# Earlier w_out conversions, and block 0's routing spread over eight ticks of block 1's layer

## Chip, cores and metric

The kernel runs on one core of a Trainium2 chip. The metric is the device time of one execution in microseconds (us), the median over the runs.

## What is computed

Three stages follow one another. Windowed attention (4 batches, 8 heads, 576 positions, head size 64) gives x with 2304 rows of 512. A gated layer with 1536 hidden units follows, and a soft mixture of 8 experts with 4 slots each.

```python
scores = np.where(masks, scale * q @ k.T, -1e9)
x = softmax(scores) @ v                                   # 2304 x 512
x = (1/(1+np.exp(-(x @ w_gate))) * (x @ w_val)) @ w_out   # 1536 hidden
logits = x @ phi                                          # 32 slots
slot_input = softmax(logits, axis=0).T @ x
slot_out = relu(slot_input @ w1[e]) @ w2[e]               # per expert e
out = softmax(logits, axis=1) @ slot_out
```

## The kernel before

The 2304 rows of x are cut into blocks 0 to 3 of 512 rows and block 4 of 256. The product with w_out is never made for x: w_out times phi is made once (`slot_weights`, into `wp`), the logits come from the hidden units g and `wp`, and g itself is gathered into the slots.

Of the gated layer a block has 12 steps f, each of 128 hidden units and two halves (`l1`: gate, then value, 12 matmuls each). Weights are split in two parts (`whl`: high and low, `split_w`, lines 492 and 493: ScalarE casts, GpSimd or VectorE subtracts). The raw weights must first be converted (`convert`, lines 438 to 441: ScalarE, VectorE twice, and an add on GpSimd, for each of two halves). Twelve conversions are for w_gate and w_val and are done along block 0's layer; six, number 12 to 17 of the order `turn`, are for w_out. The steps after which these six stand are in `WO_AT`, where 12 is the first step of block 1. Each calls `slot_weights`, whose four parts (two turns, `wt_ps`; a product, `pt_ps`; a sum, `wp_ps`) come 3 to 6 ticks later. A tick (`on_tick`) is one half of a step.

After each half `between` is called. `sab` there adds the attention of blocks 1 to 4, in 8 pairs of units: scores (`s_ps`), softmax (VectorE, ScalarE and, line 387, a scale on GpSimd), transposes (`tr`, line 187), weighted sums (`xp`, line 207). The last pair's keys are loaded into a buffer that the transposes of the pair before free.

`Post(n)` is the routing of block n, in 18 steps: logits (`lt_ps`), 12 turns of g (`tp`, line 816, four transposes each, copied into `gt` by VectorE or ScalarE in turn), weights (`dt_ps`), 3 gathers (`sp`, line 847), and the shares of the second softmax (`c_ps`, lines 873 to 890). `Spread(steps, marks)` gives out steps call by call.

Blocks 2 and 3 are done together (`pair_l1`) with sums and differences of their halves. What they need is made between block 1's layer and the pair: splits of x (`b_hi`, `b_lo`, `b`), eight sums on GpSimd (`tsum`, line 576), splits of these (`t_hl`, lines 552 and 553), and weights with their sums (`w_`, `s`, lines 612 to 640). This list, `prep`, is mixed with what is left of block 0's routing and with block 1's, so that the list ends 3 steps before the routing does. The cast at line 640 makes the high part of the second weights of the pair's first step. This stretch is called the passage below.

The order on each engine is set by a scheduler that goes by the order of the code and by when it believes an instruction's operands to be ready. The score, turn and sum matmuls of the pairs, the early loads and the prepared lists are kept in the order of the code. On each engine the instructions then run in the order given.

Of the kernel before, what the change touches and what calls it, by code (L numbers as in the profile page):

```python
# [22 lines left out]
NF = 12  # L23
HIP = 200
LA = 2
WO_AT = (12, 13, 14, 15, 16, 17)
WARM = 8
SMALL = 70
GA = 1
# [25 lines left out]
def pb_tokens(n):  # L55
    return 512 if n < 4 else 256
# [3 lines left out]
def tile_kernel(  # L60
# [25 lines left out]
    def b8(tag, shape, dt, name):  # L86
        return big.tile(shape, dt, tag=tag, name=name, bufs=BUFS[tag])
# [146 lines left out]
    def ld(ins):  # L234
        return tc.keep_in_program_order(ins) if early[0] else ins
# [172 lines left out]

    wo_at = {z: i for i, z in enumerate(WO_AT)}
    turn = [0, 1]  # L410
# [5 lines left out]
    def stage(z):  # L416
        if z in staged:
            return
        staged[z] = b8("l2", [P, 1024, 2], U32, "st")
        ld(nc.sync.dma_start(staged[z].rearrange("p a b -> p (a b)"), wd[z].bitcast(U32)))  # L420

    def store():
        while stores:
            ld(nc.sync.dma_start(*stores.pop(0)))

    def convert(z):
        i = n_conv[0]
        n_conv[0] += 1
        stage(z)
        if i + 1 < len(turn):  # L430
            stage(turn[i + 1])
        st = staged[z]
        store()
        fw = b8(("ws", "ws", "gb", "xt")[i % 4] if i < NF else ("gb", "xt")[i % 2], [P, 2, 1024], F32, "fw")
        for h in range(2):
            c = slice(512 * h, 512 * h + 512)
            top, low = fw[:, 0, c], fw[:, 1, c]
            nc.scalar.activation(top, st[:, c, 1].bitcast(F32), AF.Prelu, scale=2.0**-112, alpha=2.0**32)  # L438
            nc.vector.tensor_scalar(top.bitcast(U32), top.bitcast(U32), 3, None, ALU.logical_shift_left)
            nc.vector.tensor_scalar(low.bitcast(I32), st[:, c, 0], 2.0**-29, None, ALU.mult)  # L440
            nc.gpsimd.tensor_tensor(low.bitcast(I32), top.bitcast(I32), low.bitcast(I32), ALU.add)  # L441
        if z < NF:
            stores.append((wg32[z // 2][:, z % 2], fw[:, 1]))
        else:
            y = z - NF
            stores.append((wo32[y // 2][:, 2 * (y % 2) : 2 * (y % 2) + 2].rearrange("p a c -> p (a c)"), fw[:, 1]))
            slot_weights(2 * y, fw[:, 1].rearrange("p (c x) -> p c x", c=2), 3)
        return fw[:, 1]
# [4 lines left out]
    def on_tick():  # L453
        ticks[0] += 1
        for x in [x for x in later if x[0] <= ticks[0]]:
            later.remove(x)
            x[1](*x[2])

    def slot_weights(f, wo_f, lag):

        wt = pm.rearrange("p a b -> p (a b)").rearrange("p (k c x) -> p k c x", k=ND, c=2)
        at_ = {}

        def turned(c):
            wt_ps = ps_a.tile([P, ND, P], F32, tag="a", name="wt_ps")
            for kc in range(ND):
                nc.tensor.transpose(wt_ps[:, kc], wo_f[:, c, P * kc : P * kc + P], ident)  # L467
            nc.scalar.copy(wt[:, :, c], wt_ps)

        def product():  # L470
            pt_ps = ps_m.tile([P, 2, P], F32, tag="m", name="pt_ps")
            for kc in range(ND):
                nc.tensor.matmul(
                    pt_ps[32 * kc : 32 * kc + 32], lhsT=phi[:, kc, :], rhs=wt[:, kc], start=True, stop=True
                )
            at_["pt"] = cpool.tile([P, 2, P], F32, tag="pt", name="pt")
            nc.vector.tensor_copy(at_["pt"], pt_ps)

        def summed():
            wp_ps = ps_m.tile([P, 2, 32], F32, tag="m", name="wp_ps")  # L480
            for c in range(2):
                nc.tensor.matmul(wp_ps[:, c], lhsT=at_["pt"][:, c], rhs=i4, start=True, stop=True)
            nc.vector.tensor_copy(wp[:, f : f + 2], wp_ps)

        for n, (step, *args) in enumerate(((turned, 0), (turned, 1), (product,), (summed,))):
            later.append((ticks[0] + lag + n, step, args))

    def split_w(src, pool=(True, False)):
        whl = b8("w", [P, 2, 2, ND, P], F32R, "whl")
        src = src.rearrange("p (a k c) -> p a k c", a=2, k=ND)  # L490
        for h in range(2):
            nc.scalar.copy(whl[:, 0, h], src[:, h])  # L492
            (nc.gpsimd if pool[h] else nc.vector).tensor_tensor(  # L493
                whl[:, 1, h], src[:, h], whl[:, 0, h].bitcast(F32), ALU.subtract
            )
        return whl
# [17 lines left out]
    def l1(n, f, whl, between):  # L514
        nt = pb_tokens(n)
        per = 2048 // nt
        tag = {0: "ga", 1: "gb", 4: "xt" if f < per else "xb"}[n]
        if (n, f // per) not in g_cur:
            g_cur[n, f // per] = b8(tag, [P, per, nt], F32, "g")
        g = g_cur[n, f // per][:, f % per]  # L520
        for a in range(2):
            pt = ps_l1.tile([P, 512], F32, tag="l1", name="l1ps")
            first = True
            for dc in HP_ORDER:
                for w_, x_ in ((0, x_hi), (0, x_lo), (1, x_hi)):
                    nc.tensor.matmul(  # L526
                        pt[:, 0:nt],
                        lhsT=whl[:, w_, a, dc, :],
                        rhs=x_[n][:, dc, :],
                        start=first,  # L530
                        stop=(dc == HP_ORDER[-1] and w_ == 1),
                    )
                    first = False
            with tc.high_priority(offset=HIP):
                if a == 0:
                    nc.scalar.activation(g, pt[:, 0:nt], AF.Sigmoid)  # L536
                else:
                    nc.vector.tensor_tensor(g, pt[:, 0:nt], g, ALU.mult)  # L538
            between()
        g_sb[n, f] = g  # L540
# [401 lines left out]
    def ahead(z):  # L942
        if z < NF:
            conv[z] = convert(z)

    for z, (fn, *args) in enumerate(first_attn(lambda: stage(0))):
        fn(*args)
        if z == C0:
            sab = Pairs()
# [5 lines left out]
    def load_w(z):  # L955
        if z < NF // 2:
            wst[z] = b8("ws", [P, 2, 1024], F32, "wst")
            ld(nc.sync.dma_start(wst[z], wg32[z]))

    for f in range(NF):  # L960
        whl = split_w(conv.pop(f), SPL)
        ahead(f + LA)
        if f >= 10:
            store()
            load_w(f - 10)
        l1(0, f, whl, sab)
    after = Post(0).all()
    n0 = len(after)
    mix0 = Spread(after, [(4, 12)])

    def beside():
        sab()
# [4 lines left out]
    for f in range(NF):  # L977
        whl = split_w(wst[f // 2][:, f % 2])
# [42 lines left out]
    after = after[mix0.done :] + Post(1).all()  # L1021
# [22 lines left out]
    after = Post(2).all()  # L1044
# [298 lines left out]
```

## Time and profile before

| | |
|---|---|
| median of 3 runs | 500.19 us (499.78 to 500.73) |
| profiled execution | 499.89 us, of which 498.0 are the span |
| TensorE (PE) | busy 469.9 us, 94% of the span |
| VectorE (DVE) / ScalarE (ACT) / GpSimd (POOL) | 305.1 / 251.2 / 164.0 us |
| mean granted TensorE clock | 0.986 of full speed |

Times below are from the span's start. In the profile PE is TensorE's matmuls, PEld its weight loads, DVE VectorE, ACT ScalarE, POOL GpSimd, SPq the queue of SyncE from which the loads are issued. A row of the timeline has start, duration, engine, line, operation, what is written from what, shapes, how many; in brackets the idle time before it and what ended it. An fp32 matmul with a moving operand that is not rounded counts as two instructions (a gather of four matmuls as x8).

### The profile page before, as it was taken

To read this page: it belongs to the slowest core of one execution; us is meant where nothing else is said; L and a number is where in the kernel's file an instruction comes from. 1 tells how busy PE (TensorE), PEld (TensorE's weight loads), DVE (VectorE), ACT (ScalarE), POOL (GpSimd) and SP (SyncE) were. 2 spreads that over 40 slices of the span, in tenths; PEclk is the share of its full clock that TensorE was granted. 3 is DMA by queue.
4 is the path that set the end of the run, shared out by engine and by line. 5 is a ranking of instruction groups with operands and counts; after the bars stand their busy time and mean duration, and the time that the engine had idled before them with its cause. 6 is when DMAs were issued, how large, how long until landed. Compare 5 with 4: busy or idle time off the path is not lost.

```text
span 498.0 us, 12733 instructions
## 1 busy us (share of the span) xinstructions
PE 469.9 (94%) x5476; PEld 357.0 (72%) x5476; DVE 305.1 (61%) x563; ACT 251.2 (50%) x426; POOL 164.0 (33%) x136
## 2 busy tenths in 40 slices
PE   6789999999999999999969999999999999999993
PEld 3567777878877787786547888888887989643552
DVE  3868697957667452647977656656546665521532
ACT  2466576736658462655775545554446664300232
POOL 0242555615355521344284342332312134010100
PEclk9889999999999999999999999999999999989998
DMA  8979899976988803720002220210699884678997
GB/s 332 399 256 323 312 321 325 333 266 229 347 297 286 286 3 120 289 86 3 0 0 86 84 86 1 84 63 22 217 373 423 326 350 174 243 263 359 422 394 221
DMA packets 23785, 112.13 MB, mean 225 GB/s; under 512 B 2353, under 2 KB 7217, under 8 KB 14641
## 3 DMA queue, kind: packets, MB, share of 16 engines
q1 hardware_dynamic: 23408, 111.06, 60.5%
q8 instruction: 43, 0.70, 0.6%
q10 hardware_dynamic: 320, 0.26, 0.2%
q14 instruction: 14, 0.11, 0.1%
HBM read 97.16 MB, written 14.16 MB: 224 GB/s over the span
## 4 chain that ended last, share of the span: by engine, by line
PE 82%; DVE 7%; ACT 5%; DMA 2%; issue 2%; SPq 0%; POOL 0%; DVEq 0%; POOLq 0%; ACTq 0%
PE l1ps L526 31%; PE pa L650 12%; PE pe L650 6%; PE tp L816 4%; PE xp L207 4%; PE h_ps L1109 3%; PE pd L650 3%; PE s_ps L144 3%; PE sp L847 2%; PE so_ps L1168 2%; PE lt_ps L780 2%; PE tr L187 2%; DMA qk<-qkv 1%; PE wt_ps L467 1%; DVE whl L493 1%
## 5 line engine op out<-in xcount | busy, mean ns | idle before, releaser
L526 PE MATMUL l1ps<-x_hi,whl 128*128 128x512 f32 x384 | 129.3, 403 | 2.6 <-ACT x_hi L228 2.0
L526 PEld LDWEIGHTS l1ps<-x_hi,whl 128*128 128x128 f32 x384 | 71.9, 189 | 18.9 <-ACT x_hi L228 2.7
L526 PE MATMUL l1ps<-x_lo,whl 128*128 128x512 f32 x192 | 76.1, 397 | 0.0
L441 POOL TENSOR_TENSOR fw<-fw 128x512 int32<-128x512 int32 x36 | 50.2, 1403 | 67.5 <-DVE fw L440 40.0
L526 PEld LDWEIGHTS l1ps<-x_lo,whl 128*128 128x128 f32 x192 | 36.5, 190 | 7.3 <-issue 0.4
L538 DVE TENSOR_TENSOR g<-l1ps,g 128x512 f32<-128x512 f32 (+1 forms) x36 | 21.6, 600 | 32.5 <-PE l1ps L526 32.3
L526 PE MATMUL l1ps<-x,whl 128*128 128x256 f32 x288 | 37.3, 286 | 0.0
L526 PEld LDWEIGHTS l1ps<-x,whl 128*128 128x128 f32 x288 | 35.5, 192 | 0.6 <-ACT g L536 0.2
L536 ACT ACTIVATE g<-l1ps 128x512 f32<-128x512 f32 (+1 forms) x36 | 18.9, 526 | 29.4 <-PE l1ps L526 29.2
L493 POOL TENSOR_TENSOR whl<-w,whl 128x512 fp32r<-128x512 f32 x12 | 15.9, 1326 | 51.8 <-ACT whl L492 35.7
L493 POOL TENSOR_TENSOR whl<-wst,whl 128x512 fp32r<-128x512 f32 x12 | 16.3, 1362 | 43.8 <-ACT whl L492 43.8
L816 PE MATMUL tp<-cst,g 128*128 128x128 f32 x216 | 28.0, 275 | 0.1
L438 ACT ACTIVATE fw<-st 128x512 f32<-128x512 f32 x36 | 22.7, 674 | 9.4 <-DMA st<-wd 7.4
L816 PEld LDWEIGHTS tp<-cst,g 128*128 128x128 f32 x216 | 23.9, 140 | 4.6 <-issue 3.3
L493 DVE TENSOR_TENSOR whl<-fw,whl 128x512 fp32r<-128x512 f32 x24 | 21.3, 894 | 7.8 <-ACT whl L492 7.3
L821 ACT COPY gt<-tp 128x512 f32<-128x512 f32 x27 | 15.6, 583 | 18.0 <-PE tp L816 14.8
L207 PEld LDWEIGHTS xp<-pt_ring,v 64*64 64x64 f32 x1216 | 19.6, 138 | 6.4 <-issue 4.4
L440 DVE TENSOR_SCALAR fw<-st 128x512 int32<-128x512 uint32 x36 | 20.9, 609 | 5.0 <-DMA st<-wd 3.0
L714 DVE TENSOR_TENSOR tm<-pe,tm 128x512 f32<-128x512 f32 x12 | 8.3, 691 | 24.1 <-PE pe L650 24.1
L492 ACT CAST whl<-wst 128x512 fp32r<-128x512 f32 x24 | 14.2, 619 | 17.2 <-PE l1ps L526 9.2
L492 ACT CAST whl<-fw 128x512 fp32r<-128x512 f32 x24 | 14.7, 620 | 16.2 <-POOL fw L441 12.1
L207 PE MATMUL xp<-pt_ring,v 64*64 64x32 f32 (+1 forms) x1216 | 21.0, 221 | 1.9 <-issue 1.2
(467 smaller groups left out, 985.8 us busy)
## 6 DMA issues: line engine op xcount, KB each, us to landing
ew<-w SPq DMA_DIRECT2D x32, 1024.0 KB, 8.6
st<-wd SPq DMA_DIRECT2D x18, 1024.0 KB, 9.1
wst<-wg SPq DMA_DIRECT2D x12, 1024.0 KB, 6.7
v<-qkv SPq DMA_DIRECT2D x20, 512.0 KB, 6.3
wg<-fw SPq DMA_DIRECT2D x12, 512.0 KB, 7.9
w<-wg SPq DMA_DIRECT2D x6, 1024.0 KB, 7.7
qk<-qkv SPq DMA_DIRECT2D x10, 576.0 KB, 5.7
qk<-qkv SPq DMA_DIRECT2D x8, 528.0 KB, 4.8
```

Of the source, the lines that this page charges most:

```text
L207: nc.tensor.matmul(o, lhsT=v[k, t, i, r, :], rhs=p_[k, 2 * r + t, i, 0:nq], start=True, stop=True)
L438: nc.scalar.activation(top, st[:, c, 1].bitcast(F32), AF.Prelu, scale=2.0**-112, alpha=2.0**32)
L440: nc.vector.tensor_scalar(low.bitcast(I32), st[:, c, 0], 2.0**-29, None, ALU.mult)
L441: nc.gpsimd.tensor_tensor(low.bitcast(I32), top.bitcast(I32), low.bitcast(I32), ALU.add)
L492: nc.scalar.copy(whl[:, 0, h], src[:, h])
L493: (nc.gpsimd if pool[h] else nc.vector).tensor_tensor(whl[:, 1, h], src[:, h], whl[:, 0, h].bitcast(F32), ALU.subtract)
L526: nc.tensor.matmul(pt[:, 0:nt], lhsT=whl[:, w_, a, dc, :], rhs=x_[n][:, dc, :], start=first, stop=(dc == HP_ORDER[-1] and w_ == 1),)
L536: nc.scalar.activation(g, pt[:, 0:nt], AF.Sigmoid)
L538: nc.vector.tensor_tensor(g, pt[:, 0:nt], g, ALU.mult)
L650: nc.tensor.matmul(pt, lhsT=w[:, w_, P * c : P * c + P], rhs=x_[:, c], start=first and c == 0 and w_ == 0 and x_ is hi, stop=c == 1 and w_ ...
L816: nc.tensor.transpose(tp[:, c], g_sb[self.n, 4 * q + c][:, P * j : P * j + P], ident)
L821: nc.scalar.copy(to, tp)
```

## The change

The six conversions of w_out move two steps forward: the first two now stand behind the last two steps of block 0's layer. Ticks start there too, so that the parts of `slot_weights` follow. Block 0's routing starts when the tick counter passes 20, as before; since the counter is four ahead, this is now with 8 ticks left of block 1's layer and not 4. The marks give out all 18 steps in these 8 ticks, where 12 of the 18 were given out in 4 and the other 6 stood in the passage. The list `prep` is thereby spread over 15 steps of routing and not 21.

```diff
-WO_AT = (12, 13, 14, 15, 16, 17)
+WO_AT = (10, 11, 12, 13, 14, 15)
...
+    wo_first = WO_AT[0]
+
+    def ticking():
+        sab()
+        on_tick()
+
     for f in range(NF):
         whl = split_w(conv.pop(f), SPL)
         ahead(f + LA)
         if f >= 10:
             store()
             load_w(f - 10)
-        l1(0, f, whl, sab)
+        l1(0, f, whl, sab if f < wo_first else ticking)
+        if f in wo_at:
+            convert(NF + wo_at[f])
     after = Post(0).all()
     n0 = len(after)
-    mix0 = Spread(after, [(4, 12)])
+    mix0 = Spread(after, [(8, 18)])
```

On GpSimd, at the end of block 1's layer, the order of the two kernels differs by this piece (`qk<-qk,su` is the softmax scale of the last two pairs, two units each; `whl` the low parts of the weights of steps 9 to 11; `tsum` the pair sums).

```order
 L387 TENSOR_TENSOR qk<-qk,su 128x512 x2
 L493 TENSOR_TENSOR whl<-wst,whl 128x512 x3
+L576 TENSOR_TENSOR tsum<-xf 128x512
 L387 TENSOR_TENSOR qk<-qk,su 128x512 x2
-L576 TENSOR_TENSOR tsum<-xf 128x512 x4
+L576 TENSOR_TENSOR tsum<-xf 128x512 x3
 L576 TENSOR_TENSOR tsum<-xf,tsum 128x512 x4
```

One pair sum has moved ahead of the scale of the last pair; the other seven still follow it.

On the matrix engine the same scale is waited for by the transposes at line 187. Behind the next to last weighted sums (`xp`) the changed kernel has a turn (`tp`, four transposes) and then the 12 matmuls of one half of step 10. From the middle of that half to the first gather its rows are, without the weight loads:

```order
L526 MATMUL l1ps<-x_hi,whl 128x512 x2
L526 MATMUL l1ps<-x_lo,whl 128x512
L526 MATMUL l1ps<-x_hi,whl 128x512
L826 MATMUL dt_ps<-cst,d 128x128
L526 MATMUL l1ps<-x_hi,whl 128x512
L526 MATMUL l1ps<-x_lo,whl 128x512
L526 MATMUL l1ps<-x_hi,whl 128x512 x2
L526 MATMUL l1ps<-x_lo,whl 128x512
L526 MATMUL l1ps<-x_hi,whl 128x512
L187 MATMUL tr<-cst,qk 128x128 x4
L816 MATMUL tp<-cst,g 128x128 x4
L847 MATMUL sp<-gt,dt 32x512 x4
```

Before, 29 of the 48 logits matmuls of block 0 (`lt_ps`) stood ahead of `tr`, behind all 12 matmuls of that half of the step, and behind `tr` came the other 19 and two turns.

On ScalarE, in the passage, the rows of the changed kernel from the sixth turn copy of block 1 that is ScalarE's to the cast at line 640 are:

```order
L821 COPY gt<-tp 128x512
L681 COPY tm<-pa 128x512
L630 CAST w__3334<-s 128x256
L552 CAST t_hl<-tsum 128x512 x4
L626 CAST w__3466<-wst 128x512
L629 CAST w__3466<-wst 128x256
L640 CAST w__3335<-s 128x768
L705 COPY tm<-pe 128x512
```

Before, one of the four casts of `t_hl` stood behind the cast at line 640, and the copy at line 705 ahead of it.

## Rows read from the trace of the kernel before

**Rows 1.** Windows: busy us (instructions) of PE, PEld, DVE, ACT, POOL; clock; DMA.

```profile
102.00:108.00 6.00, 6.00 (x126) 4.60 (x126) 1.52 (x3) 1.48 (x3) 0.00 (x0) 1.00 0.62 230
...
216.00:222.00 6.00, 6.00 (x125) 5.21 (x123) 1.84 (x4) 3.48 (x7) 5.00 (x4) 1.00 0.01 3
...
246.00:252.00 6.00, 3.97 (x16) 1.97 (x12) 5.18 (x12) 4.59 (x9) 2.45 (x2) 1.00 0.00 0
```

**Rows 2.** Timeline of PE, from the end of block 1's layer.

```profile
224.51 0.39 PE L526 MATMUL l1ps<-x_hi,whl 128*128 128x512 f32 x1
224.74 0.60 PE L816 MATMUL tp<-cst,g 128*128 128x128 f32 x4
225.27 1.07 PE L847 MATMUL sp<-gt,dt 128*32 128x512 f32 x8
...
228.16 1.97 PE L847 MATMUL sp<-gt,dt 128*32 128x512 f32 x16
...
232.13 2.83 PE L780 MATMUL lt_ps<-g,wp 128*32 128x128 f32 x96 [0.37 <-DVE acc L855]
...
250.18 0.73 PE L650 MATMUL pa<-t_hl,w__3316 128*128 128x512 f32 x2 [1.41 <-ACT w__3316 L640]
...
259.71 1.65 PE L650 MATMUL pa<-t_hl,w__3315 128*128 128x512 f32 x6 [1.91 <-DVE tm L717]
```

**Rows 3.** Timelines of ACT and POOL, 203 to 250.

```profile
221.07 0.65 ACT L402 CAST x<-xp 128x256 fp32r<-128x256 f32 x2 [0.93 <-PE xp L207]
...
245.47 1.66 ACT L552 CAST t_hl<-tsum 128x512 fp32r<-128x512 f32 x3
...
249.29 0.83 ACT L640 CAST w__3316<-s 128x768 fp32r<-128x768 f32 x1
...
203.05 2.53 POOL L493 TENSOR_TENSOR whl<-wst,whl 128x512 fp32r<-128x512 f32 x2 [14.89 <-ACT whl L492]
208.26 2.04 POOL L387 TENSOR_TENSOR qk<-qk,su 128x512 f32<-128x512 f32 x2 [2.68 <-DVE su L384]
216.42 5.00 POOL L576 TENSOR_TENSOR tsum<-xf 128x512 f32<-128x512 f32 x4 [6.12 <-PE tp L816]
```

**Rows 4.** DMA issues at 92.8 and 109; all loads of st.

```profile
st<-wd SPq DMA_DIRECT2D x1, 1024.0 KB, 9.1
...
wst<-wg SPq DMA_DIRECT2D x1, 1024.0 KB, 7.6
...
DMA to landing us min/median/max: 5.2/9.1/13.9
```

**Rows 5.** Timelines of SPq, POOL, PE about the end of block 0's layer.

```profile
92.81 0.37 SPq L420 DMA_DIRECT2D st<-wd  x1
...
108.95 0.97 SPq L958 DMA_DIRECT2D wst<-wg  x1
...
117.31 2.28 POOL L387 TENSOR_TENSOR sm<-sm,su 128x512 f32<-128x512 f32 x2 [1.00 <-DVE su L384]
...
121.67 0.60 PE L187 MATMUL tr<-cst,sm 128*128 128x128 f32 x4
```

**Rows 6.** Timeline of PE, 194 to 215.

```profile
194.80 0.66 PE L187 MATMUL tr<-cst,qk 128*128 128x128 f32 x4
...
200.18 0.86 PE L144 MATMUL s_ps<-qk 64*32 64x64 f32 x64
...
202.35 1.59 PE L207 MATMUL xp<-pt_ring,v 64*64 64x32 f32 x96
...
209.35 0.66 PE L187 MATMUL tr<-cst,qk 128*128 128x128 f32 x4 [0.30 <-POOL qk L387]
...
211.16 1.09 PE L816 MATMUL tp<-cst,g 128*128 128x128 f32 x8
212.01 0.47 PE L526 MATMUL l1ps<-x_hi,whl 128*128 128x512 f32 x1
...
214.86 0.60 PE L187 MATMUL tr<-cst,qk 128*128 128x128 f32 x4
```

## Prediction

> **What bounds the kernel now.** I read the windows first. In block 1's layer the matrix engine is busy in all of every 6 us window, while VectorE, ScalarE and GpSimd have room; after the layer, in the window from 246, it is busy for 3.97 of 6 us [rows 1]. So only the passage from block 1's layer to the pair of blocks 2 and 3 has idle time to win. The timeline of the matrix engine tells the edges of that passage [rows 2]. The layer's last matmul ends at 224.51 + 0.39 = 224.90. Then come what is left of block 0's routing (a turn of four transposes and one gather, four turns, two gathers), block 1's routing from 232.13, and the first pair step. That step waits 1.41 us before 250.18, for ScalarE's cast at line 640, and 1.91 us before 259.71, for VectorE. The cast at line 640 starts at 249.29 [rows 3], that is 24.4 us after the layer's end. After it the order of the engines is nearly that of before, so I take it as the gauge: what it moves, the end moves. The chain of waits runs through matrix-engine work up to there, so work that the matrix engine does earlier costs as much there as it saves here. Only its waits can change the sum.
>
> **The change part by part.**
>
> The conversions. Their instructions are the same in number. Six conversions of 4 ScalarE, VectorE and GpSimd pieces each come two steps earlier, and so do the matrix engine's transposes and products of w_out. The layer of block 0 ends in a stretch where the others do little, from 102 to 108 [rows 1]. Price nothing, and the cover is this. The first conversion's data were asked for at 92.8 and landed 9.1 us later [rows 4, 5], about 101.9, before ScalarE comes to it. The second one's load now takes the place in SP's queue in which block 1's second weight load stood; that one landed 7.6 us after its issue at about 109 [rows 4, 5], so the data are there at 116.6 to 118.1 if I take 7.6 and 9.1 as ends. GpSimd now adds half of this conversion before it scales the softmax of a pair. A cast and a shift of some 0.5 us each, an add like GpSimd's subtraction below (1.27) and a scale of 1.14 (2.28 for two [rows 5]), with a hand-over of 0.1 or more after each, put the first scaled unit about 4 us after the landing, at 120.6 to 122.1. The matrix engine wants it for the transposes that stood at 121.67 [rows 5]; it now has four transposes of w_out ahead of them (0.42) and comes at 122.1. So the cover just holds, at both ends. SP's weight load behind the store has a whole step of slack. This part: 0, and one for one if the load is later.
>
> The routing of block 0. Five turns and two of the three gathers move from the passage into the layer. Twenty transposes at 0.85 for eight, from 211.16 to 212.01 [rows 6], are 2.1; a gather is 1.0, for two take 1.97 [rows 2]; together 4.1 us of matrix-engine work that now stands before the layer's end. The logits move within the layer and cost nothing net.
>
> New waits in the layer. (1) The last pair's transposes. GpSimd now has one of the pair sums between the weights of step 11 and the softmax scale of the last pair; before, all eight sums came after it. Take the end of the earlier weighted sums (the xp matmuls, which stood at 202.35 [rows 6]) as zero. The matrix engine then does a turn (0.42) and 12 matmuls of the layer (2.85, from 212.01 to 214.86 [rows 6]) and comes to the transposes at 3.3. The other way: ScalarE empties the sums, two casts in 0.65 [rows 3], and then casts the weights, 0.55 for one (three take 1.66 [rows 3]); GpSimd subtracts them in 1.27 (two take 2.53), adds the pair sum in 1.25 (four take 5.00) and scales in 1.02 (two take 2.04) [rows 3]. That is 4.74, and five hand-overs at about 0.1 (the scale's first half ended at 209.28, and the matrix engine went on at 209.35 [rows 3, 6]) make 5.2. A wait of 1.9, where 0.30 stood before [rows 6]: plus 1.6. (2) The last pair's second keys are asked for after the transposes that stood at 194.80, and their scores ran at 200.18, 5.4 later [rows 6]. Now the matrix engine reaches them after a turn's worth (0.44), eight transposes, 12 matmuls and five transposes, 4.7. The load is nowhere shown alone: it costs 0 if it needed less than 4.7, and 0.7 if all of 5.4. I take 0.3, since the engine had work in nearly all of the 5.4.
>
> So the layer ends at 224.9 + 4.1 + 1.6 + 0.3 = 230.9.
>
> The passage, counted from the layer's end. One gather (1.0), and its bank is emptied by VectorE before block 1's logits may use it, as before 232.13 (idle 0.37 until the copy [rows 2]): logits at 1.9. They take 2.8 [rows 2]: 4.7. ScalarE, which is idle until then, now has in order two copies of turns and two casts (2.1), nine wide copies or casts at 0.52 and three short ones (5.2 together), done at 12.1. The next copy needs a buffer that the first gather of block 1 frees. Its turns are held by ScalarE's copies until 10.9; with the last turn, three products and the gather it ends at 13.1. Then ten wide ones and two short (5.8) and the cast at line 640 can start at 18.9. Its operands from VectorE are ready by 18.2 to 18.8 by the same count, so ScalarE ends last, but barely. Wide ones go by 0.52 to 0.57 apart [rows 3], which gives 18.9 to 20.0; I take 18.9, since most of the rows are at the lower end.
>
> **The sum.** The cast at line 640 comes at 230.9 + 18.9 = 249.8 and stood at 249.3: **plus 0.5 us**. The passage gives back 1.4 of idle time (24.4 less 4.1 is 20.3, against 18.9), and the layer loses 1.9 in the new waits. The profiled execution took 499.89 us (498.0 of span and 1.9 around it), 0.30 below the median, so the sum is 500.4 on its own basis and **500.7** on that of the runs.
>
> A rule bears on the largest term. The Trainium skill, "TensorE: Matmul & The Clock Gate", in the section on the architecture of the array, says that ScalarE and VectorE are strict first-in-first-out and that GpSimd is too, on each of its cores. By that rule the pair sum holds the scale up whatever is ready. The trace agrees: GpSimd sat idle before 208.26 for 2.68 us, waiting for the scale's operand, and the sums behind it did not start before 216.42. Without the rule, were a ready scale let past, the wait would shrink to about 0.6 and the sum to minus 0.8.
>
> **The rivals.**
>
> A, faster: the wait for GpSimd does not arise, because the pair sum runs in a gap before the weights' cast (ScalarE earlier, so that the sum is done when the reciprocal comes). For it: GpSimd is free for long stretches here. Against it: the sum stands behind the weights of step 11 in its queue, and these wait for a buffer that step 9 frees. Price: 1.6 back, and up to 0.7 more if VectorE's count (18.2) holds in the passage: 0.5 - 1.6 = -1.1 to -1.8, 498.4 to 499.1. It decides when that wait is under 0.5 us.
>
> B, slower: the second conversion's load. ScalarE and VectorE stand before it in order, and behind it on ScalarE stand the sigmoid that frees a bank of the layer and on VectorE the reciprocal for the softmax. It decides at 9.2 us from issue to landing; each further microsecond is one on the matrix engine. The loads of this kind took 9.1 in the median and 13.9 at most [rows 4]: 4.8 at worst, 1.5 as a middle: 502.2, and 505.5 at worst. Against it: 7.6 in this very place of the queue.
>
> C: the change moves nothing that counts. The layer grows by exactly what the passage loses and the waits stay as they are: 500.2. It lies within the forecast's own bound.
>
> **How the numbers follow.** About 0.2%, 1.0 us, is what a measurement of this kernel can tell from no change. The forecast (with C) has 0.55: its bounds are the key wait (0 to 0.7, so -0.3 to +0.4) and the passage (18.2 to 20.0, so -0.7 to +1.1), that is 499.7 to 502.2; most of it is within 1.0 of before, a fifth above. A has 0.22, nearly all faster. B has 0.23. From these: faster 0.22, same 0.43, slower 0.35. The range leaves out B's far part and A's last bit: 498.6 to 502.7.
>
> **What would show it.** In the changed kernel: block 1's last layer matmul ends near 231; the transposes of the last pair wait 1.5 to 2.2 us for line 387 of GpSimd, with one line-576 instruction just ahead of it; the conversions' loads cost the matrix engine nothing before 130; the cast at line 640 starts near 249.8, 18.9 after the layer's end; the stretch after it is as before. I am wrong if the wait is not there (A), if the matrix engine waits for line 387 near 122 (B), or if the cast at line 640 comes more than a microsecond off its 18.9.

## The result and the profile after

Over 15 runs the changed kernel took 502.86 us in the median (499.93 to 506.05), and the kernel before 500.02 us (498.93 to 502.68), over 15 runs as well. The ratio is 1.0051 with a 95% interval of 1.0027 to 1.0074: slower by 2.6 us, 1.4 to 3.7. The profiled execution of the changed kernel took 502.86 us, of which 501.0 are the span, 3.0 more than before.

The matrix engine's timeline of the changed kernel, at the places where it stands still and at the layer's end (columns as in [rows 2]):

```profile
126.52 1.38 PE L144 MATMUL s_ps<-qk 64*32 64x64 f32 x117
129.25 0.33 PE L144 MATMUL s_ps<-qk 64*32 64x64 f32 x11 [1.35 <-issue]
...
192.16 0.59 PE L139 MATMUL s_ps<-msk 128*128 128x512 bf16 x2
192.68 2.81 PE L780 MATMUL lt_ps<-g,wp 128*32 128x128 f32 x90
196.09 0.86 PE L144 MATMUL s_ps<-qk 64*32 64x64 f32 x64 [0.60 <-DMA qk<-qkv]
...
205.89 0.86 PE L144 MATMUL s_ps<-qk 64*32 64x64 f32 x64
...
217.11 0.66 PE L187 MATMUL tr<-cst,qk 128*128 128x128 f32 x4 [2.12 <-POOL qk L387]
...
232.31 0.40 PE L526 MATMUL l1ps<-x_hi,whl 128*128 128x512 f32 x1
232.63 1.06 PE L847 MATMUL sp<-gt,dt 128*32 128x512 f32 x8
```

Block 1's layer ends at 232.71, 7.8 us later than in [rows 2]. Three waits stand in it that were not there: 1.35 us in the middle of the score matmuls of a pair, between the 117th and the 118th of 128, for nothing that the profile shows ("issue"); 0.60 for the last pair's first keys; and 2.12 for the last pair's scale, where [rows 6] has 0.30. Of block 0's routing 5.2 us stood behind the layer's end before (224.90 to 230.13 [rows 2]) and 1.0 stands there now, so 4.2 us of work moved. With the three waits less those 0.30 that makes 8.0; of the first wait some 0.4 was there before as well, as the experiments show, which leaves 7.6 of the 7.8 explained.

GpSimd in the changed kernel shows what the scale stood behind:

```profile
213.07 1.30 POOL L493 TENSOR_TENSOR whl<-wst,whl 128x512 fp32r<-128x512 f32 x1 [2.75 <-ACT whl L492]
214.32 1.28 POOL L576 TENSOR_TENSOR tsum<-xf 128x512 f32<-128x512 f32 x1
215.56 2.50 POOL L387 TENSOR_TENSOR qk<-qk,su 128x512 f32<-128x512 f32 x2
```

One pair sum runs between the weights and the scale, without a gap. And ScalarE, at the gauge of the prediction:

```profile
249.06 2.19 ACT L552 CAST t_hl<-tsum 128x512 fp32r<-128x512 f32 x4
251.14 0.63 ACT L626 CAST w__3466<-wst 128x512 fp32r<-128x512 f32 x1
251.66 0.41 ACT L629 CAST w__3466<-wst 128x256 fp32r<-128x256 f32 x1
251.97 0.84 ACT L640 CAST w__3335<-s 128x768 fp32r<-128x768 f32 x1
```

The cast at line 640 starts at 251.97, 2.7 us later than in [rows 3] and 19.26 after the layer's end. The rest of the span takes 249.0 us from there, where it took 248.7. So the layer and the passage hold 2.7 of the 3.0 us of this execution.

### The profile page after: what moved, and what is told of

It reads as the page before. It is cut to its first block, busy times and chain, and to the rows that moved or that the text cites. A ratio compares the mean times of both kernels' runs of the same rounds, so it can differ in the third digit from the quotient of the medians.

```text
span 501.0 us, 12730 instructions
## 1 busy us (share of the span) xinstructions
PE 470.8 (94%) x5476; PEld 356.7 (71%) x5476; DVE 305.8 (61%) x563; ACT 250.5 (50%) x426; POOL 164.3 (33%) x136
## 4 chain that ended last, share of the span: by engine, by line
PE 69%; DMA 5%; ACT 5%; DVE 4%; issue 2%; POOL 2%; SPq 0%; ACTq 0%; DVEq 0%
PE l1ps L526 23%; PE pa L650 11%; PE pe L650 6%; PE tp L816 4%; PE h_ps L1117 3%; PE pd L650 3%; PE sp L847 3%; PE so_ps L1176 2%; DMA w<-wg 2%; PE xp L207 2%; PE lt_ps L780 2%; PE s_ps L144 2%; DMA v<-qkv 1%; PE wt_ps L467 1%; PE tr L187 1%
## 5 line engine op out<-in xcount | busy, mean ns | idle before, releaser
L441 POOL TENSOR_TENSOR fw<-fw 128x512 int32<-128x512 int32 x36 | 51.7, 1444 | 70.9 <-DVE fw L440 35.3
L536 ACT ACTIVATE g<-l1ps 128x512 f32<-128x512 f32 (+1 forms) x36 | 18.9, 526 | 30.5 <-PE l1ps L526 30.4
L816 PE MATMUL tp<-cst,g 128*128 128x128 f32 x216 | 28.9, 276 | 0.9 <-ACT gt L821 0.9
L816 PEld LDWEIGHTS tp<-cst,g 128*128 128x128 f32 x216 | 23.9, 140 | 5.5 <-issue 3.3
L439 DVE TENSOR_SCALAR fw<-fw 128x512 uint32<-128x512 uint32 x36 | 20.5, 578 | 1.9 <-ACT fw L438 1.5
```

The lines of the kernel that those rows point to most:

```text
L816: nc.tensor.transpose(tp[:, c], g_sb[self.n, 4 * q + c][:, P * j : P * j + P], ident)
```

## The experiments

### The conversions alone

```diff
-    mix0 = Spread(after, [(8, 18)])
+    mix0 = Spread(after, [(4, 12)])
...
-        if ticks[0] > 20:
+        if ticks[0] > 24:
```

> Only the conversions of w_out and their ticks come two steps earlier; block 0's routing starts with 4 ticks left and gives out 12 of 18 steps, as in the kernel before. Theory 1 (the stall of 1.35 us inside the score matmuls near 128 belongs to the conversions: they put 24 more instructions of the matrix engine ahead of that burst, so that a 16 KB block of its code ends inside it): the stall is there again, nothing else is, and the time is 1.35 us over before, 501.4. Theory 2 (the stall is an accident of the one profiled run): no stall and 500.0. Theory 3 (the conversions' loads are late for the pairs, the forecast's rival B): a wait for line 387 of GpSimd near 122 and 501.5 or more.

Measured: 501.96 us, ratio 1.0010 (0.9981 to 1.0039). The matrix engine's rows of this kernel:

```profile
126.70 1.39 PE L144 MATMUL s_ps<-qk 64*32 64x64 f32 x117
129.31 0.33 PE L144 MATMUL s_ps<-qk 64*32 64x64 f32 x11 [1.22 <-issue]
...
196.19 0.86 PE L144 MATMUL s_ps<-qk 64*32 64x64 f32 x64 [0.43 <-DMA qk<-qkv]
```

The stall after the 117th score matmul is there again, and so is the wait for the first keys: both come with the conversions and not with the routing. Two waits more stand here, against the first theory, which had said that there would be nothing else:

```profile
209.22 1.28 PE L780 MATMUL lt_ps<-g,wp 128*32 128x128 f32 x34 [0.71 <-DVE x L403]
...
211.23 0.66 PE L187 MATMUL tr<-cst,qk 128*128 128x128 f32 x4 [0.73 <-POOL qk L387]
```

The cast at line 640 starts at 251.81 in this profile, 2.5 us later than before, and 24.39 after the layer's end as before; yet the execution is only 1.3 us longer (501.21 and 499.89). The difference lies far behind the change. In six of the fourteen profiles, those of the kernel before and of the changed kernel among them, the granted clock falls near 440; in the profile of the kernel before (columns as in [rows 1]) so:

```profile
438.00:444.00 6.00, 5.78 (x33) 1.52 (x31) 0.91 (x2) 0.00 (x0) 0.28 (x1) 0.72 0.59 199
```

In these six it takes 248.5 to 249.1 us from the cast at line 640 to the end, in the other eight 246.7 to 247.5. So the end follows the gauge only where both profiles have this fall or neither has, as the two above both have.

For the keys the reason is in the order: before, parts of the w_out product stood between the transposes that free the buffer and these scores, and they are now done earlier. No transposes wait for GpSimd's scale near 122 (they run at 122.13 without a wait, and in the changed kernel at 121.94), so the second conversion's load was in time. The timed cost, 0.5 us with an interval from -1.0 to 2.0, cannot tell 1.35 from nothing.

### The routing alone

On the kernel before, with its conversions where they were:

```diff
-    mix0 = Spread(after, [(4, 12)])
+    mix0 = Spread(after, [(6, 18)])
...
-        if ticks[0] > 20:
+        if ticks[0] > 18:
```

> The other half of the change alone, as far as it goes: the conversions stand where they stood before, and block 0's routing is spread over the last six ticks of block 1's layer (six, since the last conversion's part of the product is not there earlier), all 18 steps in them. On GpSimd no pair sum stands ahead of the last pair's scale. Theory 1 (the conversions bring the stall near 128 and the keys' wait, the pair sum ahead of the scale the third loss, and the passage gains 0.9): no stall near 128, no wait for keys, less than 0.8 us before the last pair's transposes, the cast at line 640 19.0 to 19.4 us after the layer's end, and 0.5 to 1.0 us under before. Theory 2 (the spreading itself costs, whatever the conversions do): 1 us or more over before.

Measured: 499.06 us, ratio 0.9963 (0.9946 to 0.9981), 1.9 us faster than before and the lowest ratio of the study. Its rows on the matrix engine and on ScalarE:

```profile
125.61 1.45 PE L144 MATMUL s_ps<-qk 64*32 64x64 f32 x125
128.02 0.30 PE L144 MATMUL s_ps<-qk 64*32 64x64 f32 x3 [0.96 <-issue]
...
213.54 0.60 PE L187 MATMUL tr<-cst,qk 128*128 128x128 f32 x4
...
228.43 0.39 PE L526 MATMUL l1ps<-x_hi,whl 128*128 128x512 f32 x1
```

```profile
248.95 0.84 ACT L640 CAST w__3335<-s 128x768 fp32r<-128x768 f32 x1
```

The keys and the scale are not waited for, and the cast at line 640 comes 20.1 us after the layer's end (two of block 0's gathers still stand in the passage, which the expected 19.0 to 19.4 forgot). By the runs, spreading the routing is a gain, and a larger one than the 0.5 to 1.0 us expected; where it comes from is not shown, since at the cast at line 640 this profile is ahead by 0.34 us only; the rest of its 2.2 us comes after it, where the kernel before has the fall of the clock near 440 and this profile has none. The first theory had also said that there would be no stall near 128, and here is one of 0.96 us, after the 125th score matmul, in a kernel whose conversions are not moved (and one of 0.69 before 208.48, inside weighted sums, for "issue" too). Up to there the matrix engine's order is that of the kernel before. In the profile of that kernel itself the burst took 1.88 us, and 1.48 is what it takes undisturbed (below), so about 0.4 of stall is in it:

```profile
125.84 1.88 PE L144 MATMUL s_ps<-qk 64*32 64x64 f32 x128
```

### The pair sum behind the scale

```diff
-                nc.gpsimd.tensor_tensor(s, s, su[:, y].unsqueeze(2).to_broadcast([P, 8, 64]), ALU.mult)
+                scaled[0] = nc.gpsimd.tensor_tensor(s, s, su[:, y].unsqueeze(2).to_broadcast([P, 8, 64]), ALU.mult)
...
-            kp(nc.gpsimd.tensor_tensor(t[:, c], one[:, c], two[:, c], ALU.subtract))
+            with tc.issue_after(scaled[0].ins): kp(nc.gpsimd.tensor_tensor(t[:, c], one[:, c], two[:, c], ALU.subtract))
```

On the changed kernel, this exchanges that one pair sum and the scale in GpSimd's order and nothing else on any engine.

> The changed kernel with one difference in order: the pair sum that stood on GpSimd ahead of the last pair's scale stands behind it. Theory 1 (this sum holds the scale up, and the layer's end moves the end of the run): the wait before the last pair's transposes falls from 2.12 us by the sum's 1.25 to about 0.9, and the time by 1.2 to about 501.6. Theory 2 (the passage takes it back, as ScalarE's row of casts and copies ends last there): the wait falls all the same, the cast at line 640 comes 20.5 us after the layer's end and not 19.3, and the time stays at 502.8.

> The version with the scale ahead of the pair sum once more, beside the last one. Theory 1 (the scale's wait of 2.1 us, and the half clock that followed it in some runs, make up most of the loss over the stall near 128): the stall is there with 1.2 to 1.5 us, the wait for the scale is about 0.5, and the time is 0 to 1.5 us over before, and 1.5 us or more under the changed kernel. Theory 2 (the first time was a lucky draw): 2.5 us over before, like the changed kernel.

> The changed kernel itself, unedited, beside the next three on one chip. If the stall near 128 belongs to the order of its instructions, it stands again after the 117th of the 128 score matmuls with 1.2 to 1.4 us; if it was an accident of one run, it is absent. The time should again be some 2.5 us over the kernel before.

Measured: 500.03 us, ratio 0.9995 (0.9964 to 1.0026), and the second time 499.62, ratio 0.9976 (0.9956 to 0.9996). The changed kernel, taken again on another chip: 505.01, ratio 1.0071 (1.0043 to 1.0099). In the two profiles of this version the wait is 0.54 and 0.46:

```profile
220.51 0.66 PE L187 MATMUL tr<-cst,qk 128*128 128x128 f32 x4 [0.54 <-POOL qk L387]
```

```profile
216.13 0.66 PE L187 MATMUL tr<-cst,qk 128*128 128x128 f32 x4 [0.46 <-POOL qk L387]
```

The cast at line 640 stands 19.25 and 19.24 us after the layer's end, so the passage takes nothing back. Both profiled executions were longer than their medians (504.21 and 501.54 us), so the gain of the runs cannot be read from them; the first stood still for 2.01 us in block 0's layer, before 97.41. Yet the wait is only 1.6 us shorter, and the ratios, each with 0.2 to 0.3% either way, differ by 0.0056 to 0.0095 (of 502 us, 2.8 to 4.8). The windows show what may be missing (us, busy us and instructions of PE, PEld, DVE, ACT, POOL, granted clock, DMA share, GB/s). The changed kernel's first profile, with 2.12 of wait before 217.11:

```profile
212.00:218.00 6.00, 3.88 (x22) 2.92 (x21) 4.14 (x9) 3.59 (x7) 4.93 (x4) 1.00 0.62 226
218.00:224.00 6.00, 6.00 (x40) 4.44 (x39) 2.09 (x4) 1.86 (x4) 6.00 (x6) 1.00 0.39 158
```

The same kernel taken again, with 2.18 of wait before 217.64:

```profile
212.00:218.00 6.00, 3.82 (x20) 2.88 (x21) 4.69 (x10) 3.93 (x7) 4.39 (x4) 1.00 0.71 252
218.00:224.00 6.00, 6.00 (x29) 3.79 (x28) 1.38 (x2) 1.07 (x2) 6.00 (x6) 0.72 0.43 167
```

```profile
217.64 0.66 PE L187 MATMUL tr<-cst,qk 128*128 128x128 f32 x4 [2.18 <-POOL qk L387]
...
234.43 0.40 PE L526 MATMUL l1ps<-x_hi,whl 128*128 128x512 f32 x1
```

After the wait the granted clock falls: 0.72 over six microseconds, a part of them at 1.2 GHz, and 29 instructions are done where the other execution did 40. From these transposes to the layer's end it takes 17.19 us (217.64 to 234.83) and not 15.60 (217.11 to 232.71): the half clock costs 1.6 us more. With the pair sum behind the scale the same stretch has a clock of 1.00 and takes 15.6 in both profiles. Two versions below have the long wait as well: with 2.33 us of it the clock fell and the stretch took 17.15, with 2.31 it did not and the stretch took 15.61. So the fall came in two of four profiles. The Trainium skill, "TensorE: Matmul & The Clock Gate", in the section on what is actually happening, says that the clock's windows run free of the kernel, so that the point of a change varies; the two executions above, alike in order and wait and not in clock, agree. Where the clock falls in runs without a profile is not known, but the mean granted clock over the runs is 0.985 and 0.983 for the changed kernel and 0.988 twice with the scale ahead: 0.003 to 0.005 of 502 us, 1.6 to 2.5 us of work. That this is the fall behind the wait is likely and not shown, for the mean does not tell the place, and the clock falls near 440 too. Nor is it a loss against the kernel before: that one has 0.985 to 0.986 in its runs beside these, without the long wait, so the changed kernel's clock is lower by at most 0.003. The routing alone has 0.988, like the scale ahead. Why the kernel before has less is open.

### Where the stall in the scores comes from

The page of the changed kernel has this line in its part on DMA queues (packets, MB, share):

```profile
q8 instruction: 43, 0.70, 0.6%
```

The matrix engine has 5476 matmuls and as many weight loads in the profile; over 0.70 MB that is 64 bytes for one, and 256 of them in each of the 43 packets of 16 KB. I take it from this that the queue brings the engine's code. 128 score matmuls and their weight loads are one packet's worth, done in 1.48 us. One packet of q8 lies between 126.7 and 127.9 in the changed kernel, and between 125.1 and 126.2 before, where the burst starts at 126.52 and at 125.84. So the packet came after the burst's start in the one and ahead of it in the other. Two questions follow: is the place of the stall the end of a block of code, and what makes the packet late? Shifts of the code by the number of small matmuls at the start (line 118), while the matrix engine waits for its first operands:

```diff
-SMALL = 70
+SMALL = 6
```

and 62, 102 (changed kernel), and 78 (kernel before).

> The changed kernel with 6 and not 70 of the small matmuls that run at the very start, while the matrix engine waits for its first operands: 128 instructions fewer ahead of everything (half of a block of 256 that is fetched at a time). Theory 1 (the stall near 128 is a matter of where a block of code ends): it is not at this place any more, the matrix engine's scores run through there in 1.5 us, and the time is about 1.35 us less, 501.5, unless blocks now end inside another burst, whose stall would then be seen there (1 to 1.5 us each). Theory 2 (the stall comes from the loads that crowd the DMA engines there): it stays at the same place with 1 us or more, and the time at 502.8.

> The changed kernel with 102 and not 70 of the small matmuls at the start: 64 instructions more ahead of everything, a quarter of a block of code. Theory 1 (where a block of code ends): the stall near 128 is shorter or gone, since the block then ends in the first half of the burst, behind matmuls of the layer that leave the fetch its time; the time is 0.7 to 1.4 us less, 501.5 to 502.1, if no other burst is hit. Theory 2 (crowded DMA engines): the stall stays with 1 us or more, 502.8.

> The changed kernel with 62 and not 70 small matmuls at the start: 16 instructions of the matrix engine fewer, as many as the two turns of w_out put ahead of the score matmuls near 126. The blocks of code then end at that burst where they ended in the kernel before. Theory 1 (where a block of code ends): no stall inside that burst, 1.3 us less than the changed kernel. Theory 2 (crowded DMA engines): the stall stays, and the time too.

> The kernel before with 78 and not 70 small matmuls at the start, and no other edit: no conversion is moved and no load. Theory 1 (where a block of code ends): the stall now appears in this kernel too, inside the score matmuls near 126, after the 117th of 128, with 1.2 to 1.4 us, and the time is 1.3 us over before. Theory 2 (the moved loads crowd the DMA engines): no stall, 0.0.

With 62 the stall moved; with 102 the burst ran through. The matrix engine's rows, of 62 first:

```profile
130.07 1.45 PE L144 MATMUL s_ps<-qk 64*32 64x64 f32 x124
132.90 0.30 PE L144 MATMUL s_ps<-qk 64*32 64x64 f32 x4 [1.38 <-issue]
```

```profile
125.42 0.66 PE L187 MATMUL tr<-cst,sm 128*128 128x128 f32 x4 [1.04 <-POOL sm L387]
...
130.07 1.48 PE L144 MATMUL s_ps<-qk 64*32 64x64 f32 x128
```

The kernel before with 78:

```profile
127.06 1.38 PE L144 MATMUL s_ps<-qk 64*32 64x64 f32 x117
128.73 0.33 PE L144 MATMUL s_ps<-qk 64*32 64x64 f32 x11 [0.28 <-issue]
```

Eight matmuls fewer at the start, and the stall stands after the 124th and not the 117th; eight more in the kernel before, and it stands after the 117th, where the routing alone, the same code up to there without the eight, had it after the 125th. With 6 the scores near 126 have no stall, and one of 1.76 us stands inside the weighted sums at 212.66, for "issue" too. All profiles together settle the place: they have 52 stalls for "issue" on the matrix engine, and counted in matmuls and weight loads from the start, all 52 stand whole multiples of 256 apart, to within two. So the place is the end of a block of code: that is shown. (The moved turns of w_out put 16 instructions ahead of this burst, not the expected 24.) The size of the stall is not told by the place: at the same 117th matmul it is 1.0 to 1.6 us with the conversions moved and 0.28 without. It is told by the packet: wherever a stall of 0.2 us or more stands between 90 and 235 us, 21 in all, the engine goes on 1.2 to 1.6 us after the end of a packet of q8. With 78 the packet starts after 126.2 and the burst at 127.06, ahead of it again. The expected 1.3 us at 62 and at 78 were wrong in that.

As times these four say little of the stall: 504.10 us, ratio 1.0067 (1.0042 to 1.0092) with 6; 504.58, 1.0071 (1.0039 to 1.0102) with 102; 508.19, 1.0138 (1.0109 to 1.0167) with 62; and 502.96, 1.0041 (1.0016 to 1.0065) with 78 on the kernel before. Other blocks then end in other bursts (with 78, a stall of 1.00 us in weighted sums at 160.39), the start of the kernel changes, and with 6 and 62 the scheduler also set parts of block 0 in another order. With 102 the forecast's rival B shows once: 1.04 us before 125.42 for GpSimd's scale.

The two losses taken out together, as it was hoped, with 62 small matmuls and the scale ahead:

> Both at once on the changed kernel: the last pair's scale ahead of the pair sum, and 62 small matmuls. If the two losses are independent, the time is 1.6 and 1.3 us under the changed kernel, that is about the time of before (plus 0 to 0.5); with the passage's gain of about 1 us and only the wait for the last pair's keys (0.6) and 0.2 of the scale left, it could be 0.2 us under before. If the passage or the clock takes it back, it stays 1.5 us or more over before.

Measured: 507.77 us, ratio 1.0146 (1.0114 to 1.0177); 62 brings its own losses, and the stall stayed (1.11 us).

What makes the packet late was tried by taking a load out of the crowd ahead of the burst, with the matrix engine's order as it was up to the burst and through it:

```diff
-        if f % 2:
-            load_w(f // 2 + 2)
+        if f and f % 2 == 0:
+            load_w(f // 2 + 1)
```

> The changed kernel with block 1's weight loads (1 MB each) asked for one step later; the first of them then stands behind the keys and the next raw weights in the queue of loads, and not among the loads ahead of the score matmuls near 126. The order on the matrix engine is the same, and so is the place where the block of code ends. Theory 1 (the loads that crowd the DMA engines delay the fetch of the code, which starts 0.2 us after the burst does, where it starts 0.7 us ahead of it in the kernel before): the fetch starts half a microsecond or more earlier, the stall falls from 1.35 to 0.8 or less, and the time by 0.5 to 1.3 us. Theory 2 (the fetch is late for another reason): the stall stays at 1.2 to 1.5 us, and the time at 2.5 to 3.5 us over before.

> The later weight loads and the scale ahead of the pair sum, both on the changed kernel. If both losses go, what is left against before is the keys' wait (0.6) and the passage's gain (0.9): 0.3 us under before to 1 us over it. If the later loads do nothing to the stall, it comes out as the version with the scale ahead alone did, 0.3 to 1.5 us over before.

Measured: 505.58 us, ratio 1.0097 (1.0061 to 1.0133), and 505.96, ratio 1.0105 (1.0068 to 1.0141). The matrix engine's rows of the first:

```profile
126.95 1.39 PE L144 MATMUL s_ps<-qk 64*32 64x64 f32 x117
129.31 0.33 PE L144 MATMUL s_ps<-qk 64*32 64x64 f32 x11 [0.97 <-issue]
...
144.68 0.52 PE L482 MATMUL wp_ps<-cst,pt 128*128 128x32 f32 x3 [1.44 <-DVE pt L477]
```

The stall is 0.97 here and 1.63 with the scale ahead: 1 MB less in the queue does not bring the packet in time. The later loads cost more than they could give, since the parts of the w_out product then wait for VectorE (1.44 us here) and for ScalarE (1.35 near 167), and the layer for its weights (1.29 before 216.64). Crowded loads as the cause are not borne out. In the kernel before the packet starts as the engine crosses the end of the preceding block (125.17 and 125.21), in the changed kernel 2.3 us after that (126.74 and 124.42); why stays open.

## Why the prediction was right or wrong

The forecast was 500.7 us, plus 0.5. The median, 502.86, stands 2 us above it, at the very top of the range (502.7; the ratio on 500.19 gives 502.74), and the likeliest band (within 1 us of before) was missed. That the range reached so far is luck: the forecast's own bounds ended at 502.2, and the room above them was kept for rival B, which did not come. Step by step:

- The moved work, 4.1 us: right, 4.2 found.
- The last pair's transposes: the mechanism was right, a wait for GpSimd's scale behind one pair sum, 1.9 forecast and 2.12 found (the scale took 1.25 us for one unit and not 1.02). What backs it is the version with the scale ahead, where the order alone took the wait away. The row that the prediction names for it does not: the sums before 216.42 had waited 6.12 us for a turn (`PE tp L816` in [rows 3]) and not for the scale. The price, one microsecond for each of waiting, was too low by the runs: taking the sum away gained 2.8 to 4.8 us for 1.6 of wait. A fall of the clock behind the wait, 1.6 us in two of four profiles, was not in the sum and is the likely rest.
- The conversions at nothing: the loads and the scale near 122 held, as argued. What neither the sum nor the list of rivals had is the matrix engine's own code: 1.35 us in the score matmuls, 0.95 more than the kernel before has in its profile, the largest miss in the profiled execution. Its part in the timed difference is not known; the conversions alone cost 0.5 us, not told from zero.
- The keys' wait of 0.3: placed at the second unit, where there is none (205.89 has no wait), and found at the first, 0.60, since the product that used to cover it had gone.
- The passage, 18.9 after the layer's end: 19.26, within its bounds of 18.2 to 20.0, and 19.25 in the versions with the scale ahead. ScalarE ends last there, as said; its wide casts took 0.55 (2.19 for four), where the sum had 0.52.

In the profile that is 0.5 forecast, and 0.95 of code, 0.2 of scale, 0.3 of keys, 0.36 of passage and 0.15 of moved work on top: 2.5 of the 2.7 that the cast at line 640 shows. In the runs, the conversions alone (+0.10%) and the routing alone (-0.37%) together make -0.27%, the version with the scale ahead -0.05 and -0.24%: so the change without that one pair sum would have been the same or slightly faster, and the sum ahead of the scale turned it to +0.51 and +0.71%. Rival A (the wait not there, 498.4 to 499.1) came near with its price: with the wait cut to half a microsecond the two ratios give 499.0 and 499.9. This is luck in part, since these kernels have the code's stall (1.44 us in both profiles) and the keys' wait, and a mean clock above that of the kernel before, none of which A had. Rival B did not come.

## What to carry to other kernels

Where one engine is busy all the time, a wait of two microseconds on it is not priced by its length alone: look at the granted clock behind it, and over several runs, since it falls in some executions and not in others. When work is spread into a full stage, look at what the scheduler then puts ahead of a small operation that the busy engine waits for; here one line that pins a 1.3 us sum behind the scale was worth 2.8 to 4.8 us in the runs, more than anything else that was tried. Try the halves of a change apart: the half that paid, the routing, needed neither the other half nor its waits.

## What the hardware showed unexpectedly

A burst of 128 small matmuls with their weight loads (1.48 us) uses up one 16 KB block of code, and the matrix engine stood still at a block's end for 0.24 to 2.01 us, between 90 and 235 us, in 13 of 14 profiles, at a place that moves with the number of instructions ahead of it. Most of these stalls stand inside bursts of small matmuls. The Trainium skill, "Runtime: NRT & Kernel Launch", in the section on how instructions are fetched, gives the same block of 256 instructions and says that the cost of crossing into the next is mostly hidden. The traces agree so far as a profile has 43 packets and two to six stalls; a stall is not confined to bursts, though, for the longest stood before one of the layer's long matmuls, in the first profile with the scale ahead:

```profile
97.41 0.63 PE L526 MATMUL l1ps<-x_hi,whl 128*128 128x512 f32 x2 [2.01 <-issue]
```
